# Sliding-window attention and an RWKV channel mix: other transposes for q and k, other loads, and new planner constants

## The chip, the cores and the metric

The kernel runs on one NeuronCore of a Trainium2 chip, as one program. The metric is the time of one execution in microseconds (us). Before the change its median is 235.41 us over 8 runs (234.81 to 236.02). About 0.2%, or 0.5 us, is what a measurement of this kernel can tell from no change.

A core has engines that run at the same time, each in the order of its own instruction stream: TensorE (PE: matrix products, and transposes, which are products with the identity), VectorE (DVE), ScalarE (ACT), GpSimd (POOL, which here does little but issue loads) and SyncE (SP, which issues stores and crossbar transposes by DMA). They wait for each other through semaphores. PE writes only to PSUM; ACT or DVE has to copy the result to SBUF.

## The reference

Batch 8, 8 heads, 576 positions, head size 64. Causal attention with an ALiBi bias and a window of 128, then a token-shift feed-forward network on the 512 columns that the heads give:

```python
scores = scale * q @ k.T                       # per batch and head, 576 x 576
mask   = (rel >= 0) & (rel < 128)              # rel = query position - key position
scores = where(mask, scores - slope[h] * abs(rel), -1e9)
x      = softmax(scores) @ v                   # -> [8, 576, 512]
xk     = mu_k * x + (1 - mu_k) * x_prev        # x_prev: x one position earlier, zero at the first
xr     = mu_r * x + (1 - mu_r) * x_prev
kk     = maximum(xk @ w_k, 0)                  # 512 -> 1024
out    = sigmoid(xr @ w_r) * (kk * kk @ w_v)   # 1024 -> 512
```

Inputs and output are float32; the kernel computes in bf16 with float32 accumulation.

## The kernel before, in words

**Tiles.** 576 positions are 4 blocks of 128 (q0, or r in the layouts) and a tail of 64. Heads go in pairs: a group g is two heads, so 4 groups a batch and 32 in all. For one group the kernel transposes q and k to have the head dimension on the partitions, multiplies them for the blocks that the window touches (`scores`, L658, with the bias as another product, L645, for batch 0, and a multiplication by a stored mask, L685, later), takes the exponential on ACT (L672), multiplies by v (`attend`, L716; a column of ones gives the sum), divides (L722 and L727 on DVE), transposes the result back (`out_t` L754 or `out_some` L771), copies it to `xt` (L628) and makes the two mixes xk and xr (`shift`: L814, then L821 twice). Batch 0 is done in two parts, positions 0 to 255 and 256 to 575, so that the pipeline fills sooner. `channel_mix` then takes chunks of 256 to 512 positions: xk by w_k (L907), Relu on ACT (L914), a square (L880), xr by w_r (L925), tanh (L932), kk by w_v (L941), the last product on DVE (L946), and a store from SP.

**Ways for q and k to be transposed.** There are several.

- `qk_full` (L1148 to 1162): 8 transposes of 128x128 a group on PE, one copy of 1024 on ACT. Batches 2 to 4 before.
- `qk_quad` (L994 to 1015): the batch is loaded *head-major*, in runs of four positions of one head (1 KB of float32), and PE works in quarters of its array, 64x64, 32 transposes a group (four for each block n), into two PSUM tiles. Batch 1 before (`WIDE`), and the second part of batch 0 with runs of two.
- `qk_some` (L1123 to 1146): for `QM` groups at once, with half of the array (64 rows) for each transpose, 32 transposes for two groups; four copies of 512 on ACT. `QM` is 0 before, so it isn't used.
- the crossbar: SP issues eight DMA transposes a batch (`flip`, L466) from `cb` to `qx`, and PE does nothing. Batches 5 to 7 before (`XB`).

The 64 tail positions of q and k are loaded into `ts` (`tail_load`, L447: 512 runs of 256 bytes for each of q and k) and transposed for all four groups at once by four full transposes and a DVE copy (`tails`, L845), or by the crossbar for the batches in `XTT` (6 and 7). `out_flip` (L833) does the outputs of batches 6 and 7 by crossbar.

**Order.** All instructions are given to a planner (`Plan`) with assumed durations, dependences and buffers. It plays the kernel through and emits each engine's instructions in the order in which they came up; the chip then follows that order. Priorities come from `rank`: attention of group k = 4b + g has the key (k - A) x SLOPE for each engine, and a piece of channel mix has as key the mix work (in us of PE) planned before it. So a larger A draws attention ahead of mix. Work that uses the array in 64-row mode is marked `rows = (64, 64)`, and where it is `lazy` it is held back by WAIT in the hope of standing next to other 64-row work. XRL and XD hold back xr and the crossbar batches' mixes. PE fills idle time with up to 90 products on zeros (`warm`, L619), which have the lowest priority and no use for the result.

POOL issues all loads but the first in one fixed order, given by `LOADS`: v and V are the halves of batch 0's v, 2 and 3 the q and k of batch 0's second part (two groups each), t batch 0's tail, K and k the halves of w_k, R w_r, W and w the halves of w_v, and a, b, c batch 1's q and k, its tail and its v. Later batches follow in the order a, b, c. At most eight loads are under way: a ninth waits for the first to land.

The functions that the change touches follow, with the line numbers of the profile.

Of the kernel before, what the change touches and what calls it, by code (L numbers as in the profile page):

```python
# [179 lines left out]
def kernel(  # L180
# [26 lines left out]
    SM = 128 * NF  # L207
# [1 line left out]

    PE, ACT, DVE, POOL, SPE, FAB, VIR = "PE", "ACT", "DVE", "POOL", "SP", "FAB", "VIR"  # L210
    NQ, NA, NX, NV, NC = 4, 4, 3, 2, 2
    XB = range(5, B)
    XO = range(6, B)
    X0 = 16
    NWARM = 90
    LOADS = 'v23KtVkabcRWw'
    XD = 6
    OTL = 1.5
    FIN = 384
    RATE = 284.0  # L220
    WIDE = (1,)
    PART_WIDE = True
    QUAD = 0.0565
    RUN = {2: 64 * 284 / 329.0, NF: 128 * 284 / 357.0}
    FLIP = 1.25
    NO = 5
    WAIT = 2.0
    QM = 0
    OM = 1

    def XU(b, g):
        return (DVE,)

    def SQ(order):
        return (DVE,)

    XT0 = (ACT,)
    QK0 = (ACT, DVE)
# [1 line left out]
    FT = (2, 3)  # L240
    KQ = ACT
    VCUT = True
    XTT = range(6, B)
    MMASK = False
    VDEP = 1
    TCOST = 1.5
# [56 lines left out]
    def one(h):  # L303
        return uno[h.idx if h.cls == "p1" else N1 + h.idx]
# [12 lines left out]
    def act_t(n, sb=False):  # L317
        return (n + (112 if sb else 61)) / 1200.0

    def dve_t(n, fast=1):  # L320
        return (n / fast + 66) / 960.0

    AHEAD = 30.0
    A = {PE: 14.25, ACT: 4.00, DVE: 4.50, VIR: 0}
    NBIAS = 4
    XRL = 3.0
    MODE = 0
    EARLY = 0.0
    SLOPE = 4.5

    def rank(prio):

# [96 lines left out]
    def issue_t(nd):  # L429
        return 0.53 + 0.00034 * nd  # L430
# [16 lines left out]
    def tail_load(b):  # L447
        h = Hold("ts")
        g = virtual("ts", [h])
        ns = []  # L450
        for i in range(2):
            src = (q, k)[i][b, :, SM:S].rearrange("h p d -> p h d")
            ns.append(dma(POOL, 128 * TCOST, issue_t(512), lambda e, i=i, src=src: nc.gpsimd.dma_start(
                out=ts_buf[h.idx][64 * i:64 * i + 64], in_=src), [g]))
        return h, ns
# [386 lines left out]
            res.append(fab(SPE, 1.0 * rows / 128, n, (1.0, 0.9), [hx]))  # L842
        return res

    def tails(b, prio):  # L845
        htt = Hold("tt")
        hs = th[b]
        if b in XTT:
            plan.follow(last["tt"], ttg[b])
            last["tt"] = ttg[b]  # L850
            return tth[b], ttl[b]
        hp = Hold("p1")

        def emit(e):
            for g in range(G):
                nc.tensor.transpose(  # L856
                    one(hp).bitcast(BF16)[:, 128 * g:128 * g + 128],
                    ts_buf[hs.idx][:, 2 * g:2 * g + 2].rearrange("p h d -> p (h d)"), ident)

        def emit_c(e):  # L860
            copy_any(e, tt_buf[htt.idx][:, :, 0:2].rearrange("p g t c -> p g (t c)"),
                     one(hp).bitcast(BF16)[:, 0:128 * G].rearrange("p (g w) -> p g w", g=G))

        t = op(PE, 0.0565 * G, list(tl[b]) + [n_ident], prio + (0,), emit, [hp], [hs])
        g = virtual("tt", [htt])
        c = [op(DVE, dve_t(512), [t, g], prio + (0,), emit_c, (), [hp])]
        return htt, c


# [124 lines left out]
    def qk_quad(b, g, nr, buf, deps, prio, c0, hq, take, free):  # L994

        hp = [Hold("p1"), Hold("p1")]

        def emit(e):
            for n in range(2 * nr):
                for hl, r in ((0, 0), (1, 1), (1, 0), (0, 1)):  # L1000
                    rows = slice(64 * r, 64 * r + 64)
                    nc.tensor.transpose(
                        one(hp[r]).bitcast(BF16)[64 * hl:64 * hl + 64, 64 * n:64 * n + 64],
                        buf()[rows, n // nr, 2 * g + hl, n % nr], ident[rows, rows])

        t = op(PE, QUAD * 2 * nr, list(deps) + [n_ident], prio + (3,), emit,
               hp + ([hq] if take else []), free)
        t.rows, t.lazy = (64, 64), True
        w = 64 * nr
        ys = [op(QK0 if b == 0 else ACT, {ACT: act_t(2 * w), DVE: dve_t(2 * w)}, [t], prio + (3,),  # L1010
                 lambda e, r=r: copy_any(
            e, qk_buf[hq.idx][:, :, c0 + w * r:c0 + w * r + w].rearrange("p t (c r) -> p t c r", r=nr),
            one(hp[r]).bitcast(BF16)[:, 0:2 * w].rearrange("p (t r c) -> p t c r", t=2, r=nr)),
                 (), [hp[r]]) for r in range(2)]
        return hq, ys
# [235 lines left out]
```

The softmax here doesn't subtract the row's maximum and nothing guards it: scores larger than these inputs give would overflow.

## Time and profile before

| | |
|---|---|
| median of 8 runs | 235.41 us (234.81 to 236.02) |
| the profiled execution | 235.57 us |
| its span, first to last instruction | 233.7 us |
| granted TensorE clock, mean | 1.000 |
| PE, DVE, ACT, POOL busy | 226.2, 189.3, 160.8, 97.7 us |
| transposes L1154 (qk_full) | 96, in 12 groups |
| loads, POOL's queue | 102,736 packets, 16.26 MB written |
| packets under 512 bytes | 120,056 of 131,100 |

A group line of the profile gives source line, engine, operation, tiles, shape, count, then busy time and the mean duration of one. Products on PE are pipelined, so one that the profile shows with 0.2 us may start 30 ns after the one before it; what a group costs PE is read from where the next group starts. A timeline line is start, length, engine, line and operands, and in brackets the idle time before it with what ended it. The chain of waits is followed back from the last instruction, and its lines are start, length and what held it. In the tables of windows the columns are the window, its length, and for each engine the busy time and the number of instructions, then the granted clock, the mean number of busy microseconds of the DMA engines and their rate.

### The profile page before, as it was taken

How to read it: one execution, taken by the hardware profiler on the slowest of the kernel's cores; microseconds unless marked ns; L12 is line 12 of the kernel's file. 1: busy time of each engine (PE TensorE's matmuls, PEld its weight loads, DVE VectorE, ACT ScalarE, POOL GpSimd, SP SyncE). 2: the span in 40 equal slices, each digit the busy share in tenths (PEclk: the TensorE clock that was granted, in tenths of full speed). 3: DMA queues.
4: the chain of work that ended last, by engine and by line, in shares of the span. 5: the costliest groups of instructions: out<-in, count | busy, mean ns of one | idle time of the engine just before them, and what ended most of it. 6: DMA issues, size and time to landing. Idle time of an engine off the chain costs nothing.

```text
span 233.7 us, 6268 instructions
## 1 busy us (share of the span) xinstructions
PE 226.2 (97%) x2487; PEld 136.3 (58%) x2487; DVE 189.3 (81%) x427; ACT 160.8 (69%) x292; POOL 97.7 (42%) x124
## 2 busy tenths in 40 slices
PE   8899989999999999999999999999999999999994
PEld 7476766556575765555555755454655744445462
DVE  7487978987897999989989979985869996974242
ACT  3579999759998987984984975947594726326251
POOL 8857674896894794059608745200000000000000
PEclk9999999999999999999999999999999999999999
DMA  6999999999999999589998999997242124121122
GB/s 158 177 171 195 163 169 184 150 194 203 147 143 174 113 144 196 112 109 162 204 180 110 106 197 182 181 129 168 73 98 93 45 48 146 45 91 48 62 72 90
DMA packets 131100, 31.73 MB, mean 136 GB/s; under 512 B 120056, under 2 KB 127232, under 8 KB 131072
## 3 DMA queue, kind: packets, MB, share of 16 engines
q0 software_dynamic: 102736, 16.26, 101.9%
q1 hardware_dynamic: 26592, 14.50, 26.3%
q10 hardware_dynamic: 1744, 0.59, 1.0%
q8 instruction: 19, 0.31, 0.6%
q14 instruction: 9, 0.07, 0.1%
HBM read 33.56 MB, written 9.44 MB: 184 GB/s over the span
## 4 chain that ended last, share of the span: by engine, by line
PE 84%; DMA 6%; ACT 5%; issue 2%; DVE 1%; POOL 0%; DVEq 0%; POOLq 0%; ACTq 0%
PE uno L941 27%; PE uno L907 26%; PE uno L925 14%; PE duo L716 6%; PE duo L658 5%; DMA ts<-in_k_dram 4%; DMA vs<-in_v_dram 3%; PE uno L771 2%; PE uno L1154 2%; ACT at L672 2%; ACT mask L1088 1%; ACT qk L628 1%; PE uno L856 1%; ACT rl L914 1%; ACT xt L628 1%
## 5 line engine op out<-in xcount | busy, mean ns | idle before, releaser
L941 PE MATMUL uno<-wv_sb,kk 128*128 128x512 bf16 (+2 forms) x296 | 71.8, 374 | 0.0
L907 PE MATMUL uno<-xk,wk_sb 128*128 128x256 bf16 (+2 forms) x416 | 69.5, 314 | 0.7 <-ACT rl L914 0.4
L672 ACT ACTIVATE at<-duo 128x1024 bf16<-128x1024 f32 (+2 forms) x68 | 65.7, 1002 | 5.4 <-PE duo L658 5.3
L914 ACT ACTIVATE rl<-uno 128x256 bf16<-128x256 f32 (+2 forms) x104 | 47.2, 492 | 20.3 <-PE uno L907 19.0
L907 PEld LDWEIGHTS <-wk_sb 128*128 128x128 bf16 x416 | 38.7, 98 | 22.1 <-issue 0.9
L685 DVE TENSOR_TENSOR at<-at,mask 128x1024 bf16<-128x1024 bf16 x56 | 37.8, 681 | 8.1 <-ACT at L672 7.8
L941 PEld LDWEIGHTS <-kk 128*128 128x128 bf16 x296 | 26.4, 98 | 26.2
L438 POOL DMA_DIRECT2D vs<-in_v_dram x32 | 28.3, 896 | 30.8 <-PE duo L716 27.5
L880 DVE TENSOR_TENSOR kk<-rl 128x256 bf16<-128x256 bf16 (+2 forms) x104 | 33.0, 336 | 9.4 <-ACT rl L914 8.0
L932 ACT ACTIVATE rs<-uno 128x512 bf16<-128x512 f32 x36 | 22.1, 614 | 26.1 <-PE uno L925 23.1
L925 PE MATMUL uno<-wr_sb,xr 128*128 128x512 bf16 x144 | 37.0, 379 | 0.5 <-ACT rl L914 0.5
L946 DVE SCALAR_TENSOR_TENSOR ot<-rs,uno 128x512 f32<-128x512 bf16 (+2 forms) x37 | 24.7, 669 | 12.1 <-PE uno L941 9.7
L716 PEld LDWEIGHTS <-at 128*128 128x128 bf16 x576 | 21.8, 98 | 6.0 <-issue 0.9
L821 DVE SCALAR_TENSOR_TENSOR xk<-dl,mu_sb,xt 128x576 bf16<-128x576 bf16 (+1 forms) x32 | 24.9, 782 | 0.4
L463 POOL DMA_DIRECT2D cb<-in_k_dram x24 | 21.3, 901 | 8.2 <-DMA vs<-in_v_dram 3.6
L821 DVE SCALAR_TENSOR_TENSOR xr<-dl,mu_sb,xt 128x576 bf16<-128x576 bf16 (+1 forms) x32 | 24.5, 771 | 0.0
L628 ACT COPY xt<-uno 128x256 bf16<-128x256 bf16 (+1 forms) x48 | 17.1, 405 | 9.0 <-PE uno L771 8.8
L925 PEld LDWEIGHTS <-xr 128*128 128x128 bf16 x144 | 13.5, 98 | 14.6 <-issue 0.7
L463 POOL DMA_DIRECT2D cb<-in_q_dram x24 | 21.2, 913 | 1.7 <-DMA vs<-in_v_dram 1.7
L628 ACT COPY qk<-uno 128x1024 bf16<-128x1024 bf16 (+2 forms) x26 | 18.8, 777 | 2.7 <-PE uno L1049 1.0
L716 PE MATMUL duo<-vs,at 128*128 128x65 bf16 x448 | 19.1, 193 | 0.0
L814 DVE TENSOR_TENSOR dl<-xt 128x576 bf16<-128x576 bf16 (+1 forms) x32 | 13.8, 435 | 4.2 <-ACT xt L628 4.2
(78 smaller groups left out, 207.5 us busy)
## 6 DMA issues: line engine op xcount, KB each, us to landing
out_dram<-ot SPq DMA_DIRECT2D x30, 256.0 KB, 5.1
vs<-in_v_dram POOLq DMA_DIRECT2D x32, 128.0 KB, 6.9
cb<-in_q_dram POOLq DMA_DIRECT2D x24, 128.0 KB, 7.4
cb<-in_k_dram POOLq DMA_DIRECT2D x24, 128.0 KB, 7.3
out_dram<-ot SPq DMA_DIRECT2D x10, 128.0 KB, 1.8
wk_sb<-in_moe_w_k_dram POOLq DMA_DIRECT2D x2, 512.0 KB, 8.9
wv_sb<-in_moe_w_v_dram POOLq DMA_DIRECT2D x2, 512.0 KB, 11.1
qx<-in_k_dram ACTq DMA_DIRECT2D x4, 128.0 KB, 4.9
```

The lines of the kernel that those rows point to most:

```text
L438: return dma(POOL, 256, issue_t(1024), lambda e: nc.gpsimd.dma_start(out=vs_buf[h.idx][:, j, :, 0:D], in_=v[b, :, 128 * j:128 * j + 128].r ...
L463: return [dma(POOL, 256, issue_t(1024), lambda e, r=r: nc.gpsimd.dma_start(out=cb_buf[h.idx][:, i, r], in_=src[:, :, r]), [g]) for r in ra ...
L628: (nc.scalar.copy if e == ACT else nc.vector.tensor_copy)(out=out, in_=in_)
L672: lambda e, ah=ah, w=w, hp=hp: nc.scalar.activation(out=ah(), in_=two(hp)[:, :, 0:w], func=AF.Exp, scale=float(scale)), (), [hp])
L685: nc.vector.tensor_tensor(out=a, in0=a, in1=m, op=ALU.mult)
L716: nc.tensor.matmul(a[:, hl, t - t0], lhsT=at[:, lo:lo + 128], rhs=vs[:, u, 2 * g + hl, :] if u < NF else tvb[:, 2 * g + hl], start=(u == u ...
L821: lambda e: nc.vector.scalar_tensor_tensor(out=buf[hk.idx][:, g, e0 + c0:e0 + c1], in0=dls(), scalar=mu[:, g:g + 1], in1=xc(1), op0=ALU.mu ...
L880: nc.vector.tensor_tensor(out=out, in0=in_, in1=in_, op=ALU.mult)
L907: nc.tensor.matmul(one(hp)[:, 0:n], lhsT=wk_sb[:, po, 128 * fo:128 * fo + 128], rhs=xk_buf[hx.idx][:, po, c0:c1], start=(po == 0), stop=(p ...
L914: a = op(ACT, act_t(n), [s], pr, lambda e, hp=hp, hr=hr: nc.scalar.activation(out=rl_buf[hr.idx][:, 0:n], in_=one(hp)[:, 0:n], func=AF.Rel ...
L925: nc.tensor.matmul(one(hp), lhsT=xr_buf[hx.idx][:, po, 128 * c:128 * c + 128], rhs=wr_sb[:, po], start=(po == 0), stop=(po == NPO - 1))
L941: nc.tensor.matmul(one(hv)[:, a:b], lhsT=kk_buf[hk.idx][:, fo, o:o + 128], rhs=wv_sb[:, fo, a:b], start=(fo == 0), stop=(fo == NFO - 1))
```

## The change

It makes batches 2 and 3 head-major too (`WIDE`), does q and k of batches 4 and 5 by half-array transposes for two groups at once (`QM = 2`; batch 5 was done by crossbar, `XB`), loads the tails of batches 0 and 1 in runs of four positions, 1 KB (`TW`), and transposes them by 16 products with the identity with 64 output partitions each and two DVE copies of 256 (`tails_full` keeps the old four transposes and one copy for the other batches), sends the tails of batches 4 and 5 through the crossbar (`XTT`), puts w_k's first half ahead of the loads 2 and 3 and w_r ahead of batch 1's v (`LOADS`), lets DVE take copies of head-major q and k (`QK1`) and ACT take squares of the first three chunks (`SQ`), and gives the planner other assumptions (`QUAD`, `RUN`) and other priorities (`A`, `SLOPE`, `WAIT`, `XRL`, `XD`). What is computed stays the same.

```diff
-    XB = range(5, B)
+    XB = range(6, B)
...
-    LOADS = 'v23KtVkabcRWw'
-    XD = 6
+    LOADS = 'vK23tVkabRcWw'
+    XD = 4
...
-    WIDE = (1,)
+    WIDE = (1, 2, 3)
     PART_WIDE = True
-    QUAD = 0.0565
-    RUN = {2: 64 * 284 / 329.0, NF: 128 * 284 / 357.0}
+    QK1 = (ACT, DVE)
+    TW = (0, 1)
+    QUAD = 0.040
+    RUN = {2: 64 * 284 / 345.0, NF: 128 * 284 / 390.0}
...
-    WAIT = 2.0
-    QM = 0
+    WAIT = 1.0
+    QM = 2
...
     def SQ(order):
-        return (DVE,)
+        return (DVE, ACT) if order < 3 else (DVE,)
...
-    XTT = range(6, B)
+    XTT = range(4, B)
...
-    A = {PE: 14.25, ACT: 4.00, DVE: 4.50, VIR: 0}
+    A = {PE: 7.75, ACT: 4.50, DVE: 4.00, VIR: 0}
     NBIAS = 4
-    XRL = 3.0
+    XRL = 4.0
...
-    SLOPE = 4.5
+    SLOPE = 4.7
...
+        if b in TW:
+            for i in range(2):
+                ns.append(dma(POOL, 104, issue_t(128), lambda e, i=i: nc.gpsimd.dma_start(
+                    out=ts_buf[h.idx].rearrange("p h d -> p (h d)")[:, 256 * i:256 * i + 256],
+                    in_=(q, k)[i][b, :, SM:S].rearrange("h (c r) d -> h c (r d)", r=4)), [g]))
+            return h, ns
...
+        if b not in TW:
+            return tails_full(b, prio, htt, hs)
         hp = Hold("p1")
 
         def emit(e):
...
+            for n in range(8):
+                for hl in range(2):
+                    nc.tensor.matmul(
+                        one(hp)[64 * hl:64 * hl + 64, 64 * n:64 * n + 64],
+                        lhsT=ts_buf[hs.idx][:, n],
+                        rhs=ident.rearrange("p (g t c) -> p t g c", g=G, t=2)[:, hl],
+                        start=True, stop=True)
...
+        c = [op(DVE, dve_t(256), [t, g], prio + (0,), lambda e, i=i: copy_any(
+            e, tt_buf[htt.idx][:, :, i].rearrange("p g (c r) -> p g c r", r=4),
+            one(hp)[:, 256 * i:256 * i + 256].rearrange("p (r g c) -> p g c r", r=4, g=G)),
+                (), [hp]) for i in range(2)]
...
-        ys = [op(QK0 if b == 0 else ACT, {ACT: act_t(2 * w), DVE: dve_t(2 * w)}, [t], prio + (3,),
+        ys = [op(QK0 if b == 0 else QK1, {ACT: act_t(2 * w), DVE: dve_t(2 * w)}, [t], prio + (3,),
```

More of the change, by code (lines that the diff above doesn't have):

```diff
@@ L843, in out_flip, with tails_full @@
         return res
[L845 to L851, printed above, removed]
+    def tails_full(b, prio, htt, hs):
         hp = Hold("p1")
@@ L866, in tails, with emit @@
         c = [op(DVE, dve_t(512), [t, g], prio + (0,), emit_c, (), [hp])]
+        return htt, c
+    def tails(b, prio):
+        htt = Hold("tt")
+        hs = th[b]
+        if b in XTT:
+            plan.follow(last["tt"], ttg[b])
+            last["tt"] = ttg[b]
+            return tth[b], ttl[b]
+        if b not in TW:
+            return tails_full(b, prio, htt, hs)
+        hp = Hold("p1")
+        def emit(e):
+            for n in range(8):
[5 more added lines that the diff above has]
+                        start=True, stop=True)
+        t = op(PE, 0.03 * 16, list(tl[b]) + [n_ident], prio + (0,), emit, [hp], [hs])
+        g = virtual("tt", [htt])
+        c = [op(DVE, dve_t(256), [t, g], prio + (0,), lambda e, i=i: copy_any(
+            e, tt_buf[htt.idx][:, :, i].rearrange("p g (c r) -> p g c r", r=4),
+            one(hp)[:, 256 * i:256 * i + 256].rearrange("p (r g c) -> p g c r", r=4, g=G)),
+                (), [hp]) for i in range(2)]
         return htt, c
```

## The prediction

> **What bounds the kernel now.** I read the page's busy times and slices first, to see which engine is full and when.
>
> ```profile
> span 233.7 us, 6268 instructions
> ...
> PE 226.2 (97%) x2487; PEld 136.3 (58%) x2487; DVE 189.3 (81%) x427; ACT 160.8 (69%) x292; POOL 97.7 (42%) x124
> ...
> DVE  7487978987897999989989979985869996974242
> ACT  3579999759998987984984975947594726326251
> ```
>
> TensorE (PE) is the full engine, but the share is an average, so the second view is the table of windows, cut where the character of the span changes (microseconds, busy time of PE, PEld, DVE, ACT and POOL with instruction counts, granted clock, DMA engines, GB/s).
>
> ```profile
> 9.00:40.00 31.00, 28.80 (x560) 20.99 (x559) 24.84 (x74) 26.75 (x61) 20.83 (x26) 1.00 1.83 178
> 40.00:60.00 20.00, 19.79 (x216) 11.49 (x216) 17.48 (x32) 15.09 (x26) 15.71 (x19) 1.00 2.14 180
> 60.00:190.00 130.00, 129.93 (x1442) 77.23 (x1439) 115.97 (x239) 97.82 (x170) 53.67 (x64) 1.00 1.41 136
> 190.00:234.00 44.00, 40.49 (x220) 21.00 (x217) 25.29 (x51) 17.16 (x33) 0.00 (x0) 1.00 0.24 80
> ```
>
> From 60 to 190 PE idles 0.07 us. There, only less PE work can help, and a load, a queue or a copy on another engine is hidden until it makes PE wait. All the slack lies before 40 us, and more of it than the 2.2 us that the window shows, because the warm-up matmuls (L619) are fillers that count as busy. The same windows for that line alone (PE and PEld):
>
> ```profile
> 9.00:20.00 11.00, 3.57 (x44) 2.68 (x44) 1.00 1.84 180
> 20.00:30.00 10.00, 1.06 (x13) 0.77 (x13) 1.00 2.09 168
> ```
>
> 57 fillers, 56 ns apart where they are back to back, are 3.2 us, so the front could give 5.4 us at most. The third view is the chain of waits there (start, length, what), beside POOL's timeline:
>
> ```profile
> 8.97 8.27 DMA ts<-in_k_dram
> ...
> 17.29 0.40 PE uno L856 x4
> ...
> 18.68 1.30 ACT at L672 x2
> ...
> 26.43 1.56 PE uno L907 x12
> ...
> 53.40 0.46 PE uno L1154 x8
> ```
> ```profile
> 8.97 0.69 POOL L453 DMA_DIRECT2D ts<-in_k_dram  x1 [0.42 <-DMA vs<-in_v_dram]
> ...
> 16.18 0.75 POOL L434 DMA_DIRECT2D cb<-in_k_dram  x1 [2.22 <-DMA wk_sb<-in_moe_w_k_dram]
> ```
>
> The load of batch 0's tail lands at 17.24, then ACT holds the chain to 26.4 (exponentials, masks, copies), then PE. POOL waits for the first half of wk until 16. The PE timeline prices what the change does to transposes:
>
> ```profile
> 19.11 0.61 PE L907 MATMUL uno<-xk,wk_sb 128*128 128x256 bf16 x4
> ...
> 33.00 0.45 PE L1002 MATMUL uno<-ident,cb 64*64 64x64 bf16 x32
> 33.38 1.05 PE L907 MATMUL uno<-xk,wk_sb 128*128 128x256 bf16 x8
> ...
> 41.62 0.32 PE L771 MATMUL uno<-ident,xu 64*128 64x64 bf16 x10
> 41.78 0.55 PE L658 MATMUL duo<-qk 64*128 64x256 bf16 x8
> ```
>
> Starts matter here, not durations: 10 half transposes take 41.78 - 41.62 = 0.16 us, 32 quarter ones 0.38 with the way back to full-array work.
>
> **The change, part by part.** *PE work of q and k.* Now 12 groups (batches 2 to 4) of 8 full transposes (L1154) cost 0.45 each on the chain: 5.4 us. Batch 5 costs PE nothing. After: batches 2 and 3, 8 groups of 32 quarter transposes. Starts come four to 31.7 ns in the 33.00 block, so 0.25 each, 2.0. Batches 4 and 5, 4 pairs of groups, 32 half transposes each at 14.5 ns (29 ns a pair of starts in the L771 block): 0.46 each, 1.9. These 12 blocks work in a 64-row array. Entering and leaving it costs about 0.10 and 0.12 us (the L771 block at 39.54 needs 0.25 up to the next L925, the one at 41.62 followed by more 64-row work only 0.16), so 0 when a block sits beside scores, 0.22 when it stands alone: 0 to 2.6, and I take half, 1.3. The tail transposes of batches 4 and 5 (8 at 56 ns) leave PE: -0.45. Tails of batches 0 and 1: 4 full transposes (0.22) become 16 products of 64 columns. No row has this form. Bounds are the 3.6 ns that a start costs beside its three neighbours in L1002 and the 56 ns of a full transpose; the half transposes are nearest, 14.5 ns, 0.23, with a possible switch of 0.22. That is 0.2 more in all for two, between -0.3 and 1.8. Sum: -5.4 + 2.0 + 1.9 + 1.3 - 0.45 + 0.2 = about -0.4 us, from -2.2 (all blocks joined) to +2.4 (none joined, dear tails).
>
> The Trainium skill, page "TensorE: Matmul & The Clock Gate", section "Wait — 56ns, not 53.3ns?", speaks against this part: start-to-start never drops below about 25 ns, however small the matmul. By it a quad group would cost 0.80 instead of 0.25 and a half pair 0.80 instead of 0.46, 5.8 us more in all, and the change would be slower by over 3 us. The starts above are four to 31.7 ns in this trace, so the measurement decides for array quarters.
>
> *Tail load of batches 0 and 1.* The pair for batch 0 now takes from wk's landing (7.08 + 8.9 by the table of issues, 15.9) to 17.24, 1.3 us. Batch 1's head-major loads move twice those bytes each in 1 KB runs and release POOL at 23.12 and 24.46, 1.34 apart, so the new pair should take 0.67: -0.67. Against it, one copy of 512 (0.41, DVE tt) becomes two strided ones of 256 (two such qk copies take 0.76): +0.35. Net -0.3 on the chain. POOL issues (0.7 each) get shorter, but landings set this stretch, not issues.
>
> *Order of loads.* wk's first half goes ahead of the four loads of batch 0's second part. It takes 15.9 - 12.4 = 3.4 us (the last part load is issued at 6.34 and needs 6.1), so it lands near 12.5, and the part loads near 13.7 to 15.9 instead of 10.2 to 12.4. The first channel mix (L907, 19.11 now) then waits only for batch 0's first part, whose last xk ends at 18.5 because part 1's transposes, copies and exponentials are mixed in (from 11.48). Worked by its own chain (exponential done 12.5, attend, reciprocal, product, transpose, copy, two DVE steps, some 3 us) it could end at 15.5. The 25 fillers after 15.7 (12, 5 and 8 in the timeline) are what mix can then replace: -1.4. The price is part 1's first transpose near 14.9 instead of 11.48. Part 1's third and fourth groups start at 15.95 and 17.61 now and hardly move; the first two do, by 1 to 3 us, and ACT, idle 3.0 us between 9 and 18 but 97% and 95% busy from 20 to 40, must catch up. Between 0 and +3.4; I take +0.9, since half of the groups keep their time and ACT has some of its idle time left. wr ahead of batch 1's v pushes that v by about 1.9 less the 1.3 that two tails save; its attend starts at 36.84 and v is there at 34, so nothing. If the front gains over 2.8 us, v and then wv (41.0 now) are late next, which caps the front's gain near 3.
>
> *Copies and squares.* Batch 1's eight copies of 512 (618 ns on ACT, 4.9 us in all between 26 and 39) may go to DVE, as may squares of the first three mixes to ACT. PE's waits of over 0.15 us between 26 and 40 sum to 1.6 (0.36, 0.17, 0.55, 0.48), most behind ACT. I take half, -0.8, between 0 and -1.6. Later, batches 2 and 3 add 0.2 us a group to ACT (two of 618 for one of 1042) and batch 5 adds 5 us, under PE's cover: ACT has 32 us free between 60 and 190, DVE 14.
>
> *Wide loads, POOL and SP.* Batches 2 and 3 issue 4 loads of about 0.75 for 8 of 0.90: 4.2 us of POOL each. SP loses batch 5's eight crossbar transposes and gains two for tails (6.3 to landing). Batch 4's tail is issued at 71.2 and used at 99, so that is covered; without cover each would cost 6.3 once, and stores queued behind it on SP as much. I cost all this at nothing.
>
> *Priorities* (A, SLOPE, WAIT, XRL, XD). Attention of batch 5 gets its turn at 58 us of mix work, (20 - 7.75) x 4.7, instead of 26; its mix comes at 94. Nothing as long as that lead holds: bounds -0.07 (all of the idle time) and +1.5 (a wait like the front's, 0.5, three times).
>
> Sum: -0.4 - 0.3 - 1.4 + 0.9 - 0.8 = -2.0. The profiled execution took 235.57 (span 233.7 and 1.9 around it), 0.16 above the median of 235.41. So the median to come is 233.4.
>
> **Rivals.** (a) *Part 1 comes late* and decides the other way. ACT at 97% in 20 to 30 cannot catch up, so the delay of 3.4 goes through to the first mix of part 1 (31.05 now), while the mix that was pulled ahead only fills time that part 1 no longer uses. For it: ACT holds the chain from 18 to 26. Against: the tail, at 17.24, gates part 1 today anyway. Price 3.4 - 0.4 - 0.3 - 0.8 - 0.9 of filler used = +1.0, 236.4; it decides once the delay passes what the rest gains, about 2.5. (b) *The later attention starves PE* between 60 and 190, with DVE 89% full and up to 10 us of copies added (24 at 0.41): +1.5 with a sum that gains half (-1.0), 235.9. Against: 14 us of DVE idle, lead of 36. (c) *The loads change nothing*, as ACT paces the front: ledger and tails only, -0.7, 234.7; or, where all 12 blocks stand alone (ledger +0.9) and the front gives half of its 1.6, +0.1, 235.5.
>
> **How the numbers follow.** Forecast 0.58 (231.0 to 234.9 its own range: the best ends of ledger and copies, 2.6 beyond the sum, reach 230.8; the other end is a gain of 0.5), (a) 0.20, (b) 0.10, (c) 0.12. A measurement here tells about 0.2%, 0.5 us, from no change. (c) splits 0.04 faster, 0.06 same, 0.02 slower. So faster 0.62, same 0.06, slower 0.32. The range 231.0 to 236.8 takes in (a), (b) and (c) at their prices and leaves out the far ends.
>
> **What would show it.** Right: L907 starts before 17; fewer than 35 fillers after 9; quad groups of batches 2 and 3 in 0.25 to 0.47; no L1154; PE idle in 60 to 190 below 0.3; 8 more quarter blocks and 4 half blocks, most of them beside L658. Wrong: PE waiting for ACT or for the part loads before 30; a PE wait for xk or xr after 60; blocks alone in 64-row mode; the TW products at 56 ns.

## The result, and the profile after

The changed kernel takes 237.83 us (median of 11 runs, 236.60 to 239.85) against 235.47 for the kernel before, measured beside it (32 runs). The ratio is 1.0094, 95% interval 1.0072 to 1.0117: 0.9% slower, where 233.4 was forecast. It lies outside the range (231.0 to 236.8) and has the other sign. The profiled execution took 238.25 us.

The page's busy times and slices of the changed kernel, as shown of before:

```profile
span 236.3 us, 6881 instructions
...
PE 226.6 (96%) x2791; PEld 135.0 (57%) x2791; DVE 191.0 (81%) x419; ACT 166.5 (70%) x320; POOL 89.6 (38%) x116
...
PE   7899999969989999999999999999999999999994
...
DVE  7577997959789999998898898977679985894252
ACT  3569998948977969969976994957575736326251
```

PE is as busy as before (226.6 against 226.2), and the span is 2.6 us longer. PE's ninth digit, a 6, is the place (47 to 53 us). The windows say so more exactly (microseconds, then busy time of PE, PEld, DVE, ACT, POOL):

```profile
9.00:40.00 31.00, 29.81 (x581) 21.01 (x579) 25.33 (x67) 27.51 (x68) 19.81 (x26) 1.00 1.73 181
40.00:60.00 20.00, 17.24 (x319) 10.70 (x318) 16.86 (x30) 14.93 (x29) 12.78 (x16) 1.00 1.80 195
60.00:190.00 130.00, 129.21 (x1587) 75.45 (x1584) 115.89 (x234) 102.18 (x187) 49.47 (x59) 1.00 1.31 126
```

In 40 to 60 us PE idles 2.76 us, where it idled 0.21. DVE and ACT are not fuller there than before (16.86 and 14.93 against 17.48 and 15.09), so PE doesn't wait because some engine ran out of time on average. From 60 to 190 PE idles 0.79 instead of 0.07. The fillers of the front (L619 before, L627 now):

```profile
9.00:20.00 11.00, 3.39 (x44) 2.56 (x43) 1.00 1.73 176
20.00:30.00 10.00, 0.89 (x10) 0.60 (x10) 1.00 1.54 190
```

54 fillers instead of 57. The count alone says little: each order emits all 90 that it may, the last at 24.7 us before and 24.6 after. What moved is their place: behind 15.7 us there are 11 instead of 25, and more of them stand before it, where the second part of batch 0 (part 1) now comes later.

**A ledger of PE.** I added up, from the trace, the time from each PE start to the next, and called a wait what exceeds the tile's own rate (56, 109, 162 and 216 ns for 128, 256, 384 and 512 columns, as these start one after the other in both traces, with 0.095 us for a change of the tile's shape, in rows or columns, as nearly all of the 107 changes before and the 128 after take above that rate) by more than 60 ns. Durations in microseconds:

| | before | after | after, store buffers in rotation | the best kernel below |
|---|---|---|---|---|
| PE's work | 223.5 | 223.5 | 223.5 | 221.7 |
| waits before 40 us | 5.0 | 3.8 | 4.3 | 4.0 |
| waits 40 to 70 us | 0.4 | 4.4 | 2.6 | 1.5 |
| waits after 70 us | 0.4 | 0.2 | 0.2 | 0.5 |
| span | 233.7 | 236.3 | 235.1 | 232.1 |

So the change leaves PE's work as it was (executions of one order differ by 0.4 to 0.5 in it: 223.1 in before_rotate), takes 1.2 from the waits of the front, and pays 4.0 between 40 and 70 us: with 0.2 less behind 70, +2.6, the difference of the spans. The front's 1.2 is one execution against one, and executions of one order differ there by up to 0.9 (last section); the 4.0 is far beyond that. The waits view of the changed kernel names who ends them (total, times, longest; PE, then DVE):

```profile
PE uno L779 <- DVE ot L976: 1.2, 1, 1.2
...
PE uno L971 <- DVE tt L636: 0.8, 1, 0.8
PE uno L955 <- ACT qk L636: 0.5, 2, 0.4
PE duo L724 <- ACT at L680: 0.5, 1, 0.5
PE uno L1032 <- DVE ot L976: 0.4, 1, 0.4
```
```profile
DVE ot L976 <- DMA out_dram<-ot: 2.3, 1, 2.3
```

An output product on DVE stands 2.3 us on a *store*. The chain of the changed kernel there (start, length, what):

```profile
43.27 0.61 DVE ot L976
43.89 7.23 DMA out_dram<-ot
51.21 0.69 DVE ot L976
51.90 0.73 DVE xu L735
52.63 0.34 DVE tt L636
53.02 1.02 PE uno L971 x4
```

The product at 51.21 writes the buffer whose store was issued at 43.89 and landed 7.23 us later. DVE works in order, so the copy of the tails (`tt`) stands behind it. PE waits 1.2 us for that product and 0.8 for that copy: L779 and L971 need neither as an input, but they write a PSUM bank that has to be read out first. In the kernel before, no DVE product waits for a store; its four stores issued between 45 and 54 us took 4.9 to 5.9 us.

### The profile page after: what moved, and what is told of

Read it like the earlier page. It is cut to its first block, busy times and chain, and to the rows that moved or that the text cites. A ratio compares the mean times of both kernels' runs of the same rounds, so it can differ in the third digit from the quotient of the medians.

```text
span 236.3 us, 6881 instructions
## 1 busy us (share of the span) xinstructions
PE 226.6 (96%) x2791; PEld 135.0 (57%) x2791; DVE 191.0 (81%) x419; ACT 166.5 (70%) x320; POOL 89.6 (38%) x116
## 4 chain that ended last, share of the span: by engine, by line
PE 78%; DMA 9%; DVE 4%; ACT 4%; issue 1%; POOL 1%; DVEq 0%; POOLq 0%; ACTq 0%
PE uno L971 25%; PE uno L937 23%; PE uno L955 11%; PE duo L666 6%; PE duo L724 6%; DMA tv<-in_v_dram 4%; DMA out_dram<-ot 3%; PE uno L779 3%; DMA vs<-in_v_dram 3%; ACT rl L944 1%; PE duo L653 1%; DVE xk L829 1%; DVE ot L976 1%; PE uno L724 1%; PE uno L627 1%
## 5 line engine op out<-in xcount | busy, mean ns | idle before, releaser
L971 PE MATMUL uno<-wv_sb,kk 128*128 128x512 bf16 (+2 forms) x296 | 72.7, 374 | 1.0 <-DVE tt L636 0.8
L937 PE MATMUL uno<-xk,wk_sb 128*128 128x256 bf16 (+2 forms) x416 | 70.3, 314 | 0.4 <-ACT qk L636 0.3
L944 ACT ACTIVATE rl<-uno 128x256 bf16<-128x256 f32 (+2 forms) x104 | 48.5, 501 | 22.7 <-PE uno L937 21.6
L937 PEld LDWEIGHTS <-wk_sb 128*128 128x128 bf16 x416 | 38.6, 98 | 22.3 <-issue 0.7
L971 PEld LDWEIGHTS <-kk 128*128 128x128 bf16 x296 | 26.2, 98 | 27.3 <-issue 1.2
L910 DVE TENSOR_TENSOR kk<-rl 128x256 bf16<-128x256 bf16 (+2 forms) x89 | 29.3, 344 | 10.8 <-ACT rl L944 9.7
L955 PE MATMUL uno<-wr_sb,xr 128*128 128x512 bf16 x144 | 36.8, 379 | 0.5 <-ACT qk L636 0.5
L976 DVE SCALAR_TENSOR_TENSOR ot<-rs,uno 128x512 f32<-128x512 bf16 (+2 forms) x37 | 24.6, 669 | 12.9 <-PE uno L971 8.1
L724 PEld LDWEIGHTS <-at 128*128 128x128 bf16 x576 | 22.0, 98 | 7.3 <-issue 2.2
L829 DVE SCALAR_TENSOR_TENSOR xk<-dl,mu_sb,xt 128x576 bf16<-128x576 bf16 (+1 forms) x32 | 24.6, 779 | 0.4
L636 ACT COPY qk<-uno 128x512 bf16<-128x512 bf16 (+1 forms) x39 | 20.7, 598 | 3.5 <-PE uno L1032 2.7
L636 ACT COPY xt<-uno 128x256 bf16<-128x256 bf16 (+1 forms) x48 | 17.4, 421 | 7.3 <-PE uno L779 6.4
L955 PEld LDWEIGHTS <-xr 128*128 128x128 bf16 x144 | 13.7, 98 | 14.8 <-issue 0.5
L724 PE MATMUL duo<-vs,at 128*128 128x65 bf16 x448 | 19.2, 193 | 0.5 <-ACT at L680 0.5
L471 POOL DMA_DIRECT2D cb<-in_q_dram x16 | 14.1, 899 | 7.2 <-PE uno L779 6.4
L735 DVE TENSOR_TENSOR xu<-duo,rc 128x640 bf16<-128x640 f32 x20 | 16.4, 819 | 0.2
```

The costliest lines, as they stand in the source:

```text
L636: (nc.scalar.copy if e == ACT else nc.vector.tensor_copy)(out=out, in_=in_)
L724: nc.tensor.matmul(a[:, hl, t - t0], lhsT=at[:, lo:lo + 128], rhs=vs[:, u, 2 * g + hl, :] if u < NF else tvb[:, 2 * g + hl], start=(u == u ...
L829: lambda e: nc.vector.scalar_tensor_tensor(out=buf[hk.idx][:, g, e0 + c0:e0 + c1], in0=dls(), scalar=mu[:, g:g + 1], in1=xc(1), op0=ALU.mu ...
L910: nc.vector.tensor_tensor(out=out, in0=in_, in1=in_, op=ALU.mult)
L937: nc.tensor.matmul(one(hp)[:, 0:n], lhsT=wk_sb[:, po, 128 * fo:128 * fo + 128], rhs=xk_buf[hx.idx][:, po, c0:c1], start=(po == 0), stop=(p ...
L944: a = op(ACT, act_t(n), [s], pr, lambda e, hp=hp, hr=hr: nc.scalar.activation(out=rl_buf[hr.idx][:, 0:n], in_=one(hp)[:, 0:n], func=AF.Rel ...
```

## The experiments

**1. Is it the store's buffer?** The planner takes the lowest free number of five output buffers, so a buffer is used again as soon as the planner believes its store done (by its constants about 4 us from the start of the issue: 0.6 for the issue, 1.0 until the transfer, 0.8 for it, and `OTL`, 1.5). In rotation the longest free one is taken. Nothing else moves: every engine keeps its order row for row. The same edit in the kernel before is the control.

```diff
-            return min(free) if free else None
+            return min(free, key=lambda a: self.given.get(a, a - 99) if h.cls == "ot" else a) if free else None
...
-            self.free[h.cls].add(h.idx + i)
+            self.free[h.cls].add(h.idx + i) or h.cls != "ot" or self.given.update({h.idx: 1 + max(self.given.values(), default=0)})
```

> The changed kernel with one difference: the output buffer ot is taken in rotation (the one given back longest ago) instead of the lowest free number. The order of PE, POOL and ACT work stays row for row the same. Theory S (the third output product waits for the first store to land, because it reuses ot buffer 0 after the planner's 4.2 us while the store takes 7.2): the DVE wait of 2.3 us for the store goes, PE's waits between 48 and 57 shrink from 3.4 to below 1.2, the median falls by 1.5 to 3 us, to about 235 to 236. Rival A (ACT is what is late there, the store only stands in front of it): the waits move to ACT qk and ACT at, and the median stays within 0.8 us of 237.8.

> The kernel before with the same rotation of ot. Theory S: it never waits for a store (its first reuse of a buffer comes later), so 235.4 within 0.4 us. Rival (rotation is good by itself, for every kernel): faster by over 1 us.

Measured: 237.09 us, ratio 1.0058 (1.0037 to 1.0079), and for the kernel before 0.9994 (0.9977 to 1.0010). The wait on the store is gone, and instruction by instruction the trace gains 1.8 us after 40 us; a front that landed 0.55 later in that execution hides part of it. In the times the store's part is 0.36 of the 0.94%, about 0.8 us; the two intervals overlap a little, so its size is rough. Theory S named the wait rightly and its worth too high: the median (237.09) is 0.7 below the changed kernel's, within what rival A allowed, and PE's waits between 48 and 57 us fall from 3.3 to 1.8, not below 1.2. The rest is something else; what follows on the changed kernel starts from the one in rotation.

**2. Undoing one part at a time.** Each run takes one part back, or puts one part into the kernel before.

```diff
# oldloads
-    LOADS = 'vK23tVkabRcWw'
+    LOADS = 'v23KtVkabcRWw'
# oldcopies
-    QK1 = (ACT, DVE)
+    QK1 = ACT
-        return (DVE, ACT) if order < 3 else (DVE,)
+        return (DVE,)
# wide1
-    WIDE = (1, 2, 3)
+    WIDE = (1,)
# oldprio
-    XD = 4
+    XD = 6
-    WAIT = 1.0
+    WAIT = 2.0
-    A = {PE: 7.75, ACT: 4.50, DVE: 4.00, VIR: 0}
+    A = {PE: 14.25, ACT: 4.00, DVE: 4.50, VIR: 0}
-    XRL = 4.0
+    XRL = 3.0
-    SLOPE = 4.7
+    SLOPE = 4.5
# before_halves
-    QM = 0
+    QM = 2
# before_wide
-    WIDE = (1,)
+    WIDE = (1, 2, 3)
```

> The changed kernel with rotation and the load order of before (w_k's first half behind loads 2 and 3, w_r behind batch 1's v). Theory: w_k early gives nothing, since the first channel mix starts at 19.3 in the changed kernel against 19.1 before, with as many fillers; so within 0.8 us of the rotated kernel, mix starting at 19 to 20. Rival L (w_k first pays, or costs, what the prediction said): 1.4 us slower, or 1 us faster.

> The changed kernel with rotation, squares on DVE alone and head-major q and k copies on ACT alone, as before. Rival A (squares given to ACT crowd it between 20 and 70, where it is 97% busy, and PE waits for its copies): 1 us or more faster than the rotated kernel. Theory of the prediction (sharing the copies helps by 0.8): 0.5 to 1.5 us slower.

> The changed kernel with rotation, but batches 2 and 3 not head-major: they take half-array transposes for two groups, as batches 4 and 5 do. Theory P (a quarter-array block of one group holds two of the four PSUM banks until two copies of 512 are done, and the output product, w_r's product and the next block then wait for a bank between 48 and 67): half as many blocks, so PE's waits between 40 and 70 fall from 2.8 to about 1.5 and the median to 235.5 to 236.5. Rival (order of attention and mix is what starves PE there): waits stay at 2.5 or more, 237 or slower.

> The changed kernel with rotation and the old priorities (A, SLOPE, XRL, WAIT, XD). Rival O (the later attention makes the waits of 48 to 67): these waits below 1 us, 235.5 or faster. Theory P: the blocks of batches 2 and 3 still need two banks each and come earlier, beside the first mix: waits of 2 us or more before 70, 236.5 or slower.

> The kernel before with one difference: q and k of batches 2 to 4 by half-array transposes, two groups at once. The ledger says PE work of 12 x 0.45 = 5.4 us becomes 6 blocks of 0.46 and a switch of 0.1 on the average, 3.4: 2.0 us less, so 233.4 if no wait comes. Theory P: six blocks hold two banks each, where twelve held one: waits of up to 1 us, 233.4 to 234.5. Rival: waits of over 2 us, no gain.

> The kernel before with one difference: batches 2 and 3 head-major (loads in 1 KB runs, quarter-array blocks, copies on ACT). Ledger: 8 x 0.45 = 3.6 us becomes 8 x (0.25 + 0 to 0.22), so 0 to 1.6 less PE work. Theory P: new waits between 45 and 70 of 2 us or more behind PSUM banks, so 235.5 to 238. Rival (the blocks are harmless, something else in the change makes the waits): 234 to 235.2 with waits there below 0.6.

| kernel | median, us | ratio to before (95%) | a large sum of PE's waits with one cause, us |
|---|---|---|---|
| after_rotate (for comparison) | 237.09 | 1.0058 (1.0037 to 1.0079) | 1.1, behind DVE ot |
| oldloads | 237.91 | 1.0085 (1.0064 to 1.0106) | 1.3 (two waits), behind ACT rl |
| oldcopies | 241.65 | 1.0252 (1.0229 to 1.0275) | 1.8, behind DVE xk, at 213 us |
| wide1 | 242.69 | 1.0327 (1.0311 to 1.0344) | 1.8, behind DVE xk, at 215 us |
| oldprio | 238.93 | 1.0160 (1.0146 to 1.0173) | 1.1 (two), behind ACT qk |
| before_halves | 237.56 | 1.0105 (1.0090 to 1.0120) | 1.3 (three), behind ACT rl |
| before_wide | 240.63 | 1.0222 (1.0203 to 1.0241) | 2.6, behind the load of `ts` |

By its median every mixture is slower than the kernel that it was made from, all but oldloads by more than the intervals. Two, oldcopies and before_wide, lie outside both lines expected of them. That can't be the price of the parts: wide loads of batches 2 and 3 can't cost 2% both where they are added and where they are left out. One constant makes the planner write another order for the whole kernel, and new waits stand far from the part that was touched (213 us in oldcopies, which changes copies of batches 1 to 3 and squares of the first mixes). The one line that shows what such an order hangs on, from the waits of before_wide:

```profile
PE uno L856 <- DMA ts<-in_k_dram: 2.6, 1, 2.6
```

It is at 91 us; the kernel before has no wait of PE on a load after 40 us. So these runs tell that parts and order belong together, and not what a part costs. The next experiments keep the order that the planner wrote and change only what is emitted.

**3. Is K ahead of the part loads a gain?** Only POOL's queue changes, in both directions.

```diff
# ar_klate: the changed kernel, rotation, w_k's first half behind the four part loads
+        pool = [n for n in done if n.eng == POOL and n.emit is not None]
+        done.remove(pool[4])
+        done.insert(done.index(pool[8]) + 1, pool[4])
...
# b_kfirst: the kernel before, w_k's first half ahead of them
+        pool = [n for n in done if n.eng == POOL and n.emit is not None]
+        done.remove(pool[8])
+        done.insert(done.index(pool[3]) + 1, pool[8])
```

> The changed kernel with the output product's buffers in rotation, every instruction of PE, ACT and DVE in the same order; only POOL's queue differs: the first half of w_k is issued behind the four loads of part 1, as in the kernel before. Theory F (bringing K ahead makes part 1 and the tail late and costs about 1 us in the first 20 us): 235.9 to 236.6 against 237.1 for the same kernel with K ahead. Rival (ACT and the copies pace the front, the order of those loads is worth nothing): no change, within 0.3 us. The term of the prediction (K ahead is worth 0.5 net) would make it 237.6.

> The kernel before with one thing changed, POOL's queue: the first half of w_k is issued ahead of loads 2 and 3 of part 1; every instruction of PE, ACT and DVE in the same order. Theory F: 0.5 to 1.5 us slower (236 to 237 against 235.4). The term of the prediction: 0.5 us faster, as K comes early, provided that PE's order had work waiting for it; as the order is that of the kernel before, it can hardly use it, so a rival is no change within 0.3 us.

b_kfirst is 237.53 us, ratio 1.0091 (1.0066 to 1.0115). wk lands at 12.1 instead of 15.9, the part loads at 12.9 to 15.1 instead of 10.3 to 12.5, and the waits of PE show the price:

```profile
PE uno L1002 <- DMA qx<-in_q_dram: 1.2, 1, 1.2
...
PE uno L1002 <- DMA qx<-in_k_dram: 0.5, 1, 0.5
```

From there each DVE instruction starts 2.06 us later than in the kernel before; 0.65 of it is made up by 35 us, 1.41 stays to the end. Theory F holds in its direction for that order, which has no work waiting for an early wk; by the medians the loss (2.0 us) is beyond its 1.5, by the trace within it. In the changed kernel, whose order was written for K first, K late gives 236.63, ratio 1.0043 (1.0029 to 1.0057): the trace gains 0.39, the intervals overlap, and experiment 5 doesn't confirm it. What K's place is worth in that order stays open, within about 0.4. The forecast gain of K first isn't found in either kernel.

**4. Do the copies of quarter-array blocks hold PE's banks between 48 and 68 us?** The kernel has four single PSUM banks, `uno`. A quarter-array block needs two of them until its two copies are done (the wait of L955 at 50.1 us is on such a copy). ar_thincopy makes the copies short, ar_notails leaves a use of a bank out; which bank each instruction takes stays as planned. PE's waits in after_rotate that lie in this stretch:

```profile
PE uno L1032 <- DVE ot L976: 1.1, 1, 1.1
...
PE duo L724 <- ACT at L680: 0.4, 1, 0.4
PE uno L955 <- ACT qk L636: 0.4, 1, 0.4
...
PE uno L971 <- ACT qk L636: 0.2, 1, 0.2
```

```diff
# ar_thincopy
-        w = 64 * nr
+        w, part = 64 * nr, 8 if b in (2, 3) else 64
...
-            e, qk_buf[hq.idx][:, :, c0 + w * r:c0 + w * r + w].rearrange("p t (c r) -> p t c r", r=nr),
+            e, qk_buf[hq.idx][:, :, c0 + w * r:c0 + w * r + w].rearrange("p t (c r) -> p t c r", r=nr)[:, :, 0:part],
...
# ar_notails, in the emission of the four transposes of L858 and of their copy
+            if b in (2, 3):
+                return
```

> The changed kernel with the output product's buffers in rotation, the same order; the copies of q and k of batches 2 and 3 out of PSUM cover 8 of 64 columns, so the values of those two batches are left undone. Theory P (PE stands between 48 and 68 us because the two banks of a quarter-array block come free late, when the copies are done): its waits in 48 to 68 us go from about 2.5 to under 1, and the run to 235.1 to 236.1. Rival (the waits there come from the output products and the exponentials, which the copies don't hold): waits of 2 or more are left, and the run is within 0.5 of 237.1.

> The changed kernel with the output product's buffers in rotation, the same order; the tails of batches 2 and 3 are neither transposed nor copied (they are left out), which frees one PSUM bank and one copy of DVE at 49 and at 62 us and takes 0.44 us of work from PE. Theory P (a bank is short): the wait of about 0.5 at 49.5 goes and the later ones shrink, 235.8 to 236.4 against 237.1. Rival (ACT is late there, banks are not short): the waits stay, and only the 0.4 of PE's own work is gone, 236.7.

ar_thincopy: 235.96, ratio 1.0025 (1.0010 to 1.0040). Against after_rotate its instructions come 0.37 earlier from 52 us and 0.36 more from 69 us: the waits on the copies, at 50.1 and 66.1 there, are gone. Another 0.51 of its lead was there by 40 us and began at 17 us, where both do the same. But the largest wait is as it was (1.0 behind an output product), and 2.1 us are left: the time came out in theory P's range, the waits on the rival's side. ar_notails: 236.97, ratio 1.0073 (1.0050 to 1.0096). From 40 us on its lead over after_rotate is the same 0.67 to the end: neither the use left out nor 0.4 us less work on PE gained anything, and the wait on the copy merely grew from 0.4 to 0.7.

So the copies of these blocks are worth about 0.7 us, of which the shorter work of ACT and DVE may be a part, and they are not the main cause. That banks are short is not refuted. ar_notails can't show it, as the bank left empty goes to no other instruction while the planned numbers stay. And of the four waits above, three are for a place to write: L1032 reads `cb` and the identity, L955 reads `xr` and w_r, L971 reads `kk` and w_v, and what they wait for, an output product or a copy of q and k, writes none of these but reads a bank. By the start-to-start count they are 2.15 of 2.6 us; only L724 waits for its input, the exponential. So in this stretch PE stands mostly until DVE or ACT has read a bank out. Kernels with more banks were not tried.

**5. Is DVE's order the cause of the largest wait?** The chain of after_rotate up to it:

```profile
49.05 0.47 PE uno L1032 x32
49.52 0.58 ACT qk L636
50.10 0.04 issue
50.14 1.04 PE uno L955 x4
51.18 0.02 issue
51.20 0.60 ACT rs L962
51.80 0.60 ACT xt L636 x2
52.40 0.02 issue
52.42 0.47 DVE dl L822
52.90 0.02 issue
52.92 0.82 DVE xk L829
53.74 0.73 DVE xr L829
54.47 0.37 DVE dl L822
54.84 0.61 DVE ot L976
55.45 0.04 issue
55.49 0.45 PE uno L1032 x32
```

Read from below: the block at 55.49 waits for a bank that the output product empties; that product's sum (L971) is finished at 54.0, but DVE has a shift in front of it; the shift had waited for ACT's copies, ACT for PE, and PE for the copy of an earlier quarter-array block. Here the product goes ahead of one `xr` and one `dl`:

```diff
+        dve = [n for n in done if n.eng == DVE and n.emit is not None]
+        for n in (dve[125], dve[124]):
+            done.remove(n)
+            done.insert(done.index(dve[126]) + 1, n)
```

> The changed kernel with the output product's buffers in rotation; one change in DVE's order: the output product that PE waits for at 54 us goes ahead of one xr and the next dl. Theory Q (its input is ready at 54.0 and it is only queued behind xr and dl, till 54.75): the wait of 1.06 falls to about 0.4, and the run to 236.4 to 236.6 against 237.1. Rival (what DVE does later instead is on PE's path as well, as xk at 55.35 feeds the next mix): another wait takes its place, and the run is within 0.3 of 237.1.

> Output product ahead on DVE and w_k's first half behind the loads of part 1, both on the changed kernel with its output buffers in rotation. If the two gains are real and add up (0.4 and 0.6): 235.9 to 236.2. If the front's 0.4 was the chance landing of a load, or is eaten by a later wait: 236.4 to 236.7.

The waits of PE in ar_otfirst:

```profile
PE uno L1032 <- DVE ot L976: 0.4, 1, 0.4
...
PE uno L937 <- DVE xk L829: 0.4, 1, 0.4
```

The wait falls from 1.1 to 0.4 as theory Q has it, and the next mix then waits 0.4 for the `xk` that was moved back, by the start-to-start count 0.5. Between 40 and 70 us the run gains 0.13. The medians are 236.41, ratio 1.0045 (1.0027 to 1.0064), and 236.51, 1.0036 (1.0015 to 1.0057), with K late as well; neither can be told from after_rotate, and the two gains don't add up. The first median lies in theory Q's range as it stands, but the kernel before ran lower beside it as well (235.42 against 235.85), and the ratio falls by 0.13%, 0.3 us. So the trace speaks for the rival: PE, ACT and DVE hand one chain to each other here, and in this one move what was moved ahead delayed the next link.

**6. Do the parts cost that in any order?** Two kernels with the change's parts (quarter-array transposes of batches 1 and 2, half-array ones for two groups, batch 0's tail in wide runs, shared copies and squares, rotation), and a new order, written with loads and stores nearer to what the traces show. K stays behind the part loads, the crossbar starts from batch 5. The core of the second:

```diff
-    XB = range(6, B)
+    XB = range(5, B)
-    LOADS = 'vK23tVkabRcWw'
-    XD = 4
-    OTL = 1.5
+    LOADS = 'v23tKVkabcRWw'
+    XD = 7
+    OTL = 3.5
-    WIDE = (1, 2, 3)
+    WIDE = (1, 2)
-    TW = (0, 1)
-    QUAD = 0.040
-    RUN = {2: 64 * 284 / 345.0, NF: 128 * 284 / 390.0}
+    TW = (0,)
+    QUAD = 0.042
+    RUN = {2: 64 * 284 / 335.0, NF: 128 * 284 / 375.0}
-        return (DVE, ACT) if order < 3 else (DVE,)
+        return (DVE, ACT) if order < 4 else (DVE,)
-    XTT = range(4, B)
+    XTT = range(5, B)
-    A = {PE: 7.75, ACT: 4.50, DVE: 4.00, VIR: 0}
+    A = {PE: 8.75, ACT: 1.00, DVE: 2.25, VIR: 0}
-    EARLY = 0.0
-    SLOPE = 4.7
+    EARLY = 2.5
+    SLOPE = 4.50
-                ns.append(dma(POOL, 104, issue_t(128), lambda e, i=i: nc.gpsimd.dma_start(
+                ns.append(dma(POOL, 120, issue_t(128), lambda e, i=i: nc.gpsimd.dma_start(
```

> The changed kernel's parts (quarter-array transposes of batches 1 to 3, head-major batches 1 and 2, the tails of batch 0 in wide runs, copies of q and k shared by ACT and DVE, squares of batches 0 and 1 shared) with output buffers in rotation, w_k behind the loads of part 1, crossbar from batch 5, and an order written for slower loads (wide runs at 335 and 375 instead of 345 and 390, a tail load 120 KB, a store's buffer free 2 us later). Theory T (the parts cost nothing by themselves, the order that counted on early data did): PE's waits from 40 to 70 us under 1.5 us, 233.6 to 235.2. Rival (quarter blocks and shared copies overload ACT and DVE in 48 to 68 us in any order): waits of 2 us or more there, 235.5 to 237.

> As the last, with other priorities and the squares of batches 0 to 3 shared. Theory T: 233.3 to 234.9, waits from 40 to 70 us under 1.5. Rival: 235.5 to 237.

> The same kernel as b2_honest, once more: 234.2 to 234.8 against 235.4, a ratio of 0.995 to 0.998, if its lead was no chance of the chip; 235.2 or more if it was.

> The kernel before with output buffers in rotation, none of the change's parts, and an order written for the slower loads and stores. If the gain of b2_honest is the new order's alone: 234.0 to 234.8, level with it. If it belongs to the change's parts (PE's work 0.7 lower, and copies shared): 235.0 to 235.8, no better than the kernel before, and behind b2_honest by 0.6 or more.

| kernel | median, us | ratio to before (95%) |
|---|---|---|
| b1_honest | 234.87 | 0.9990 (0.9970 to 1.0011) |
| b2_honest | 234.43 | 0.9967 (0.9945 to 0.9989) |
| b2_again, the same kernel | 234.20 | 0.9955 (0.9941 to 0.9969) |
| bb_honest, new order, none of the parts | 236.30 | 1.0028 (0.9997 to 1.0058) |

The second kernel beats both, the changed one by over 1%. The first is level with the kernel before; by the ledger PE's waits from 40 to 70 us are 2.0 in it, where theory T said under 1.5 and the rival 2 or more, so only the second (just under 1.5) meets theory T. Its page and windows (b2_again):

```profile
span 232.1 us, 6603 instructions
...
PE 224.6 (97%) x2655; PEld 134.4 (58%) x2655; DVE 189.2 (81%) x414; ACT 163.7 (70%) x317; POOL 93.6 (40%) x120
```
```profile
40.00:60.00 20.00, 19.34 (x342) 11.53 (x343) 18.92 (x33) 16.64 (x31) 15.22 (x18) 1.00 2.15 186
60.00:190.00 130.00, 129.61 (x1478) 75.70 (x1473) 114.38 (x229) 97.92 (x181) 50.97 (x61) 1.00 1.42 135
```

PE idles 0.66 in 40 to 60 us instead of 2.76, though ACT and DVE do more there (16.6 and 18.9) than in the changed kernel. By the ledger PE's work is 1.8 lower than before and its waits 0.1 higher. So most of these parts can stand in an order with few waits. That the order alone makes the difference is not shown: from 40 to 70 us this kernel has four quarter blocks and two half-array pairs, where after_rotate has six and none.

The control is less clean. By its median the kernel before gains nothing from a new order, but its runs scatter from 234.41 to 237.24, and the profiled one was the fastest (span 232.4, waits 4.7, PE's work 223.3 as before). It got there by fewer waits, the second kernel by less work; that the lead belongs to the parts is likely, and shown only for PE's work. Which of the new prices (stores, loads, tails) the order needed was not separated either, and batches 3 and 5 go other ways in it than in the change.

## Why the prediction was wrong

- **The ledger of PE came out level, not at -0.4.** PE's work is 223.5 in both, to within some 0.5. The starts cost what was said (32 quarter starts 0.25, a half-array pair 0.46). The changes of shape cost more: each takes 0.09 to 0.10 us, and there are 21 more of them, 2.0 us, where 1.3 was taken. "0 when a block sits beside scores" holds for half-array blocks alone, which have the scores' shape (64x128). A quarter block (64x64) pays the same change beside scores as beside full-array work: the one at 71.00, which scores follow, takes 0.38 to the next start, as the one at 25.24 does. The 16 tail products took 0.37 with the way back (0.54 in batch 0, where PE stood about 0.15 in their middle until the load of k's tail had landed, at 16.74). The lines for three of these, a block beside full-array work, the tail products with their way back, and a block beside scores:

```profile
25.24 0.45 PE L1032 MATMUL uno<-ident,cb 64*64 64x64 bf16 x32
25.61 0.61 PE L937 MATMUL uno<-xk,wk_sb 128*128 128x256 bf16 x4
...
27.98 0.44 PE L885 MATMUL uno<-ident,ts 128*64 128x64 bf16 x16
28.35 0.34 PE L762 MATMUL uno<-ident,xu 128*128 128x128 bf16 x3
...
71.00 0.45 PE L1032 MATMUL uno<-ident,cb 64*64 64x64 bf16 x32
71.38 0.56 PE L666 MATMUL duo<-qk 64*128 64x256 bf16 x8
```

  32 starts in 0.37 us again contradict the floor of about 25 ns from start to start that the Trainium skill states ("TensorE: Matmul & The Clock Gate", "Wait — 56ns, not 53.3ns?"), so weighing it down there was correct; the case was lost elsewhere.

- **"Order of loads", -1.4 for fillers, failed.** The loads landed as said (wk 12.05, part loads 12.76 to 15.83), but "could end at 15.5" did not come: the fourth `xk` ended at 17.4, behind a transpose at 15.43 and ACT's copy at 15.85 that stood in line with part 1's work, and the first mix (L937) started at 19.28, not before 17; it was 19.11 before. 54 fillers are left, where under 35 (of 57) were forecast: of the 25 behind 15.7 us 14 did go, but as many came in before, while part 1 was late. The two terms together were to be -0.5. The front's waits did fall by 1.2 (0.7 in after_rotate), where the four terms for it came to 1.6, but all of that lies between 26 and 40 us (2.8 to 1.3): before 26 us, where the moved loads act, they rose by 0.3. "K first" alone lost 1.4 us by the trace and 2.0 by the medians in the kernel before, and gave nothing that could be measured in the changed one.

- **"All the slack lies before 40 us", and the terms costed at nothing on the strength of it, are the step that lost the case.** It is true of the kernel before, whose order keeps ACT and DVE ahead of PE. It says nothing of a new order. "Nothing as long as that lead holds" (priorities), "under PE's cover" (later copies) and "I cost all this at nothing" (wide loads, POOL and SP) put at zero what the trace shows as +4.0 us of waits of PE between 40 and 70 us; the bound of +1.5 was not wide enough. Of these, 1.8 went with the store buffers in rotation. The other 2.2 are mostly waits for a bank that DVE or ACT reads out late; which of the terms they belong to, priorities, copies or blocks, stays open, as experiment 2 could not part them.

- **A wait that was missed altogether: the reuse of an output buffer.** "Stores queued behind it on SP" was looked at for crossbar transposes only. DVE waits 2.3 us for a store between 49 and 51 us, about 0.8 us of the result. The first output product comes 1.3 us earlier than before (43.19 against 44.54), and the planner gave its buffer to the third. The trace of before has stores of 4.9 to 5.9 us there, and one of 8.5 issued at 127.8; set against the planner's 4, they would have shown the risk.

- **Rivals.** (b), "the later attention starves PE" between 60 and 190, named the kind of failure, with DVE as the late engine, but the wrong place: that window lost 0.7, the stretch from 40 to 60 2.6. (a), "part 1 comes late", happened (its first transpose at 14.21, 14.9 was said; the first mix of part 1 at 33.8 instead of 31.1), but PE's waits before 40 us did not grow by it. (c) is refuted by the time.

- **"Copies and squares", -0.8, came out, its cause unproven.** PE's waits of over 0.15 us between 26 and 40 us sum to 0.8 after the change, where 1.6 was counted. That the shared copies do it isn't shown: taking them back rewrote the whole order (241.65).

- **"Tail load", -0.67 for the pair of loads, was a little large.** The new pair for batch 0 lands 0.91 us behind the last part load (15.83 to 16.74), a gain of 0.4 on the 1.3 of before.

## What to carry to other kernels

A slack map holds for the order that it was read from: when a change lets a planner write a new order, every "hidden" term needs its own margin, and the first margins to look at are buffers that are freed by a transfer, whose length varies (2.0 to 8.5 us for stores of 256 KB in the trace of before). To test one part of such a change, freeze the order and alter only what is emitted; switching one constant back measured another order each time. And a tuned order is only as good as its prices: with prices moved toward what the trace shows and new priorities, most of the parts that had lost 0.9% came out 0.3 to 0.5% ahead.

## What the runs showed of the hardware that was not expected

Stores of 256 KB issued at 45 to 54 us took 4.9 to 5.9 us in the kernel before, and two issued at 43.9 and 44.5 took 7.2 and 7.3 in the changed one. Why was not tried. The windows show more bytes moved there (193 and 197 GB/s in 40 to 50 and 50 to 60 us against 167 and 193), but the longest store of before, 8.5 us from 127.8, stands where they show 144.

Runs with the same order differ by up to 0.9 us between 20 and 40 us, behind waits that loads end (at 8.1 and 17.6 us in after_rotate), and then keep the difference that they have at 40 us to the end unless something was changed behind it. So a lag that is constant from 40 us on (ar_notails) is no effect of an edit at 49 us, and one that steps at the edit (ar_thincopy, after_rotate) is.
